# Forty weight columns in place of 64 in a state update, and fixed places in a scratch tile

## The chip, the cores and the metric

The kernel runs on one core of one Trainium2 chip. The metric is the device time of one execution in microseconds (us), taken as the median of several runs. Profiles are of one execution, and their times are counted from the start of its span.

## The reference

The whole program is an attention-like recurrence over 768 steps for 4 batches of 8 heads with 40 dimensions each, followed by two layers of a mixture of eight experts over the 3,072 tokens that come out of it. Only the recurrence matters for the change:

```python
    B, H, S, D = r.shape                       # 4, 8, 768, 40
    state = np.zeros((B, H, D, D), dtype=np.float32)
    for t in range(S):
        ...
        y[:, :, t] = np.einsum('bhd,bhde->bhe', rt, state)
        Sa = np.einsum('bhde,bhe->bhd', state, at)
        state_decay = state * wt[:, :, None, :] - np.einsum('bhd,bhe->bhde', Sa, bt)
        state = state_decay + np.einsum('bhd,bhe->bhde', vt, kt)
...
    x = np.ascontiguousarray(attn_out.transpose(0, 2, 1, 3)).reshape(B * S, H * D)
    x = _moe_ref(x=x, **moe_kwargs)
    return _moe2_ref(x=x, **moe2_kwargs)
```

The experts' part takes, for each token, one of eight experts by the largest logit, runs two matrix products with a ReLU between them, and scales the result by the expert's probability.

## The kernel before

The recurrence is done in 24 chunks of 32 steps. Within a chunk everything is a matrix product: the 32 steps' corrections to each other are gathered in a triangular system, whose inverse is needed for each of the 32 pairs of batch and head. Four chunks form a group, and there are six groups (0 to 5). The inverses of a group's four chunks are worked out together on VectorE, ahead of their use.

The order of the work is written out by hand: a loop over the chunks calls small functions in fixed places (slots), and VectorE work that has time is dealt out between them by a list with budgets (`Fill`). Each engine then works through its own instructions in that order and waits on semaphores where it needs another engine's result. So a slow step holds up everything behind it on its engine.

What is touched by the change:

- `z_` (L540 to L549) is the state update of a chunk on TensorE: 16 products into the PSUM tile `zps`, each with 64 columns of the tile `kb` as weights and two runs of 40 columns of `vu` moving. A head has 40 dimensions; its weights stand in 64 places of `kb`, 16 elements apart, and the last 24 places hold zeros. Two heads share the 128 PSUM partitions, one in the rows from 0, the other in the rows from 64. Each product is executed as two passes, so the profile shows 32 weight loads and 32 matmuls a chunk.
- `z_up` (L551 to L557) runs behind it on VectorE. It adds all 128 rows of `zps` to the state `zs` and scales by the chunk's decay. The next chunk's `x_z` (L523) needs the result. The path from chunk to chunk is thus `x_z` on TensorE, a copy on ScalarE, `u_` (L534), four scalings into `vu` on ScalarE (L538), `z_` (L549), and `z_up` on VectorE (L555, L557).
- Other steps on TensorE that the text names: `r_t` (L505) and `s_t` (L564) are transposes, `y_s` (L592), `y_c` (L602) and `c_` (L583) make the chunk's output, `chunk_a` (L333, L346, L358) prepares later chunks, `v_t` (L574) transposes `vu`.
- `solve` (L368 to L406) works out the inverses of groups 2 to 5; groups 0 and 1 go through another function, `Halves`. It has 31 steps `s`, each a product into the scratch tile `pr` (`t1`, L389) and a difference of it from the inverse's rows (`t2`, L395). In 27 of the 31 steps both are cut in two halves, so that the order is first product, second product, first difference, second difference. The text calls the place between the second difference of one step and the first product of the next a **seam**; there are 26 a group between steps that are cut, 104 in all.
- `pr` is taken anew from a pool with one buffer at each step, and the second half's product stands directly behind the first's in it.

At a seam the first product needs three things of the step before: the row `s + 1` of the inverse, which the first difference writes, the place in `pr`, and the tile itself, which the pool gives again when the last reader of the old one, the second difference, is done.

Of the kernel before, what the change touches and what calls it, by code (L numbers as in the profile page):

```python
# [11 lines left out]
F32 = mybir.dt.float32  # L12
# [4 lines left out]
P = 128  # L17
B, H, S, D = 4, 8, 768, 40
# [17 lines left out]
PRES = (0, 0, 7, 15, 15)  # L36
TAIL, SPREAD, AHEAD = 42, 60, (80, 91)
# [17 lines left out]
def attention(tc, zones, ident, r, k, v, w, a, b, emit_x, hook0, hook1, hook2, hook3, unsafe, extra, tail):  # L55
    nc = tc.nc
    with ExitStack() as ctx:
        cp = ctx.enter_context(tc.tile_pool(name="a_const", bufs=1))
        wp = ctx.enter_context(tc.tile_pool(name="a_work", bufs=2))
        ps = Warm(tc, ctx.enter_context(tc.tile_pool(name="a_psum", bufs=1, space=PSUM)), ident)  # L60

# [306 lines left out]
        def solve(st):  # L368
            box = {}
# [13 lines left out]

            def t1(s, a, z):
                am, tm = box["am"], box["tm"]
                if a == s + 1:
                    box["pr"] = wp.tile([P, 256], F32, name="pr", bufs=1)
                prv = box["pr"][:, (a - s - 1) * (s + 1) : (z - s - 1) * (s + 1)].rearrange("p (t j) -> p t j", j=s + 1)
                nc.vector.tensor_mul(prv, am[:, a:z, s : s + 1].to_broadcast([P, z - a, s + 1]),  # L389
                                     tm[:, s : s + 1, : s + 1].to_broadcast([P, z - a, s + 1]))  # L390

            def t2(s, a, z):
                tm = box["tm"]
                prv = box["pr"][:, (a - s - 1) * (s + 1) : (z - s - 1) * (s + 1)].rearrange("p (t j) -> p t j", j=s + 1)
                nc.vector.tensor_sub(tm[:, a:z, : s + 1], tm[:, a:z, : s + 1], prv)  # L395
# [12 lines left out]
        class Halves:  # L408
# [10 lines left out]
            def ops(self):  # L419
                am, tm, st, n = self.am, self.tm, self.st, L // 2  # L420

                def t0():
                    self.pr = wp.tile([P, 256], F32, name="pr", bufs=1)
                    for o in (0, n):
                        nc.vector.transpose(out=am[:, o : o + n], in_=st["aa"].rearrange("p h c t -> p t (h c)")[:, o : o + n])
# [67 lines left out]
        class Chunk:  # L493
# [46 lines left out]
            def z_(self):  # L540
# [3 lines left out]
                self.zps = zps = ps.tile([P, 2, 512], F32, tag="z", name="zps", bufs=1)  # L544
                for p in range(4):
                    for vv in range(2):
                        for i2 in range(2):
                            o = zps[64 * i2 : 64 * i2 + 64, vv, 0:320].rearrange("q (u p d) -> q u p d", u=2, p=4)[:, :, p]
                            nc.tensor.matmul(out=o, lhsT=kb[:, vv, i2, :, 4 * p + c], rhs=self.vuv[:, vv, :, 4 * i2 + p, :], start=True, stop=True, skip_group_check=True)  # L549
# [1266 lines left out]
```

## Time and profile before

| | |
|---|---|
| Median of 3 runs | 1023.16 us (1020.48 to 1031.33) |
| The profiled execution's own time | 1024.33 us |
| Its span, first to last instruction | 1022.1 us |
| Busy: TensorE matmul / weight load | 906.4 us / 838.8 us |
| Busy: VectorE / ScalarE / GpSimd | 706.1 / 506.6 / 304.7 us |
| Mean granted TensorE clock | 0.947 |

The span has two parts: the recurrence, up to about 500 us, and the experts behind it. The busy times are of the whole span. They say little of the change, which lies in the first part alone: there it has to be read stage by stage which engine waits for which.

### The profile page before, as it was taken

Reading aid. Unit: us, or ns where it says so; the run is one execution under the profiler, and the core shown is the slowest. Engines: PE = TensorE matmul, PEld = TensorE weight load, DVE = VectorE, ACT = ScalarE, POOL = GpSimd, SP = SyncE. Lnnn points to the kernel's source line nnn. Section 1 sums busy time; section 2 is a strip of 40 time slices with the busy share of each in tenths; the row PEclk is TensorE's granted clock in tenths of the full one; section 3 lists DMA queues with packets and bytes.
Section 4 is the critical chain, followed back from the end, with each engine's and each line's share of the span. In section 5 each row is a group of like instructions: output and inputs, shape, how many; then the busy total and the mean of one; then the engine's idle time right before and its main releaser. Section 6 shows DMA issues by size and latency. Waiting matters only on the chain. (4 is left out here: it accounts for less than half of the span.)

```text
span 1022.1 us, 38222 instructions
## 1 busy us (share of the span) xinstructions
PE 906.4 (89%) x16089; PEld 838.8 (82%) x16089; DVE 706.1 (69%) x2022; ACT 506.6 (50%) x991; POOL 304.7 (30%) x361
## 2 busy tenths in 40 slices
PE   7747988788878888988879899999999999999995
PEld 7646777677767777766769799999999999999995
DVE  7799899998996985853545354545464776766762
ACT  6625445445445577643523254444443565665662
POOL 6550021211120211112133334543543433323321
PEclk9779979998999999998989899999999999999998
DMA  5554445433532623226017434445343111271110
GB/s 175 141 136 111 73 107 108 116 90 79 98 86 47 159 51 87 50 51 158 17 28 173 124 97 134 129 106 152 101 126 97 30 40 53 79 214 42 40 41 26
DMA packets 152421, 96.41 MB, mean 94 GB/s; under 512 B 127407, under 2 KB 139585, under 8 KB 151850
## 3 DMA queue, kind: packets, MB, share of 16 engines
q1 hardware_dynamic: 138154, 72.53, 28.3%
q0 software_dynamic: 14080, 21.28, 8.1%
q8 instruction: 130, 2.13, 0.9%
q14 instruction: 57, 0.47, 0.1%
HBM read 112.18 MB, written 14.59 MB: 124 GB/s over the span
## 5 line engine op out<-in xcount | busy, mean ns | idle before, releaser
L1293 PE MATMUL hp<-xs,h 128*128 128x256 f32 (+1 forms) x840 | 157.1, 317 | 0.0
L1304 PE MATMUL yp<-h,hh 128*114 128x320 f32 (+1 forms) x464 | 146.9, 317 | 0.3 <-DMA s<-moe_w 0.3
L1305 PE MATMUL yp<-l,hh 128*114 128x320 f32 (+1 forms) x464 | 144.2, 311 | 0.0
L1306 PE MATMUL yp<-h,hl 128*114 128x320 f32 (+1 forms) x464 | 144.0, 310 | 0.0
L1296 DVE SCALAR_TENSOR_TENSOR hl<-hp,hh 128x456 fp32r<-128x456 f32 (+1 forms) x116 | 76.6, 660 | 90.9 <-ACT hh L1295 90.9
L1293 PEld LDWEIGHTS hp<-xs,h 128*128 128x128 f32 x840 | 124.6, 190 | 3.3
L1295 ACT ACTIVATE hh<-hp 128x456 fp32r<-128x456 f32 (+1 forms) x116 | 66.5, 573 | 110.8 <-PE hp L1293 106.2
L1293 PE MATMUL hp<-xs,l 128*128 128x256 f32 (+1 forms) x504 | 102.5, 312 | 0.0
L1214 DVE TENSOR_TENSOR l<-s,h 128x768 fp32r<-128x768 f32 x88 | 80.6, 956 | 13.1 <-ACT h L1213 10.8
L1304 PEld LDWEIGHTS yp<-h,hh 128*114 128x114 f32 (+1 forms) x464 | 85.3, 184 | 0.6 <-issue 0.5
L1305 PEld LDWEIGHTS yp<-l,hh 128*114 128x114 f32 (+1 forms) x464 | 85.3, 184 | 0.2
L1306 PEld LDWEIGHTS yp<-h,hl 128*114 128x114 f32 (+1 forms) x464 | 85.1, 183 | 0.0
L1293 PEld LDWEIGHTS hp<-xs,l 128*128 128x128 f32 x504 | 80.1, 190 | 3.1
L1249 POOL DMA_INDIRECT xg<-x,le x52 | 61.9, 1190 | 69.2 <-issue 58.0
L1220 DVE TENSOR_TENSOR l<-s,h 128x640 fp32r<-128x640 f32 x88 | 72.6, 825 | 3.0 <-ACT h L1219 3.0
L1361 POOL DMA_INDIRECT out<-yo,ti x28 | 34.5, 1232 | 129.2 <-ACT yo L1357 74.7
L1213 ACT CAST h<-s 128x768 fp32r<-128x768 f32 x88 | 70.4, 835 | 1.6 <-DMA s<-moe_w 1.5
L1219 ACT CAST h<-s 128x640 fp32r<-128x640 f32 x88 | 63.3, 719 | 0.0
L389 DVE TENSOR_TENSOR pr<-z_sol 128x110 f32<-128x110 f32 (+20 forms) x232 | 58.5, 282 | 3.9
L985 POOL TENSOR_TENSOR ccnt<-ccnt,oh 128x8 bf16<-128x8 bf16 x24 | 6.7, 279 | 179.5 <-PE rp L983 145.7
L1003 POOL DMA_INDIRECT lst<-l2e,posi x32 | 40.8, 1276 | 60.9 <-DVE posi L996 53.5
L1267 DVE TENSOR_TENSOR xs<-ta,xs 128x456 fp32r<-128x456 f32 (+1 forms) x28 | 18.5, 662 | 55.2 <-ACT xs L1266 55.2
(364 smaller groups left out, 1996.2 us busy)
## 6 DMA issues: line engine op xcount, KB each, us to landing
s<-moe_w SPq DMA_DIRECT2D x22, 1280.0 KB
s<-moe_w SPq DMA_DIRECT2D x22, 1024.0 KB
s<-moe_w SPq DMA_DIRECT2D x44, 256.0 KB
z_w<-w SPq DMA_DIRECT2D x40, 160.0 KB
z_kb<-k SPq DMA_DIRECT2D x24, 160.0 KB
z_kb<-b SPq DMA_DIRECT2D x24, 160.0 KB
z_pa<-a SPq DMA_DIRECT2D x96, 40.0 KB
rt<-r SPq DMA_DIRECT2D x96, 40.0 KB
```

Of the source, the lines that this page charges most:

```text
L389: nc.vector.tensor_mul(prv, am[:, a:z, s : s + 1].to_broadcast([P, z - a, s + 1]), tm[:, s : s + 1, : s + 1].to_broadcast([P, z - a, s + 1]))
L1213: nc.scalar.copy(wt["h1"][:, :, s], wt["s1"][:, :, s])
L1214: nc.vector.tensor_sub(wt["l1"][:, :, s], wt["s1"][:, :, s], wt["h1"][:, :, s].bitcast(F32))
L1219: nc.scalar.copy(wt["h2"][:, s], wt["s2"][:, s])
L1220: nc.vector.tensor_sub(wt["l2"][:, s], wt["s2"][:, s], wt["h2"][:, s].bitcast(F32))
L1249: d = self.nc.gpsimd.indirect_dma_start(out=b.xg[:, h], out_offset=None, in_=b.lay.src, in_offset=IndirectOffsetOnAxis(ap=b.le[:, h, 0:1]. ...
L1293: nc.tensor.matmul(out=hp[:, i], lhsT=l, rhs=r, start=k == 0, stop=k == len(ops) - 1)
L1295: nc.scalar.activation(hh[:, s], hp, AF.Relu)
L1296: nc.vector.scalar_tensor_tensor(out=hl[:, s], in0=hp, scalar=0.0, in1=hh[:, s].bitcast(F32), op0=ALU.max, op1=ALU.subtract)
L1304: nc.tensor.matmul(out=yp, lhsT=hh[:, k, t], rhs=wt["h2"][:, k], start=k == 0, stop=False)
L1305: nc.tensor.matmul(out=yp, lhsT=hh[:, k, t], rhs=wt["l2"][:, k], start=False, stop=False)
L1306: nc.tensor.matmul(out=yp, lhsT=hl[:, k, t], rhs=wt["h2"][:, k], start=False, stop=k == 7)
```

## The change

Three things are changed. The products of `z_` take the first 40 of a head's 64 weight columns, and so write 40 of its 64 PSUM rows. The PSUM tile that they write, now called `zz`, is taken once at the kernel's start and set to zero there on VectorE; `z_up` still reads all 128 rows of it. And `solve` takes its scratch tile once for a group's inverses and gives the first half's products the places from 0 and the second half's the places from 128, in every step; the tile grows from 256 to 264 elements.

```diff
+PR = 264
...
+        zz = ps.tile([P, 2, 512], F32, tag="z", name="zz", bufs=1)
+        nc.vector.memset(zz[:, :, :320], 0.0)
...
+            def place(s, a, z):
+
+                if "pr" not in box:
+                    box["pr"] = wp.tile([P, PR], F32, name="pr", bufs=1)
+                o = 128 if a > s + 1 else 0
+                return box["pr"][:, o : o + (z - a) * (s + 1)].rearrange("p (t j) -> p t j", j=s + 1)
+
             def t1(s, a, z):
                 am, tm = box["am"], box["tm"]
-                if a == s + 1:
-                    box["pr"] = wp.tile([P, 256], F32, name="pr", bufs=1)
-                prv = box["pr"][:, (a - s - 1) * (s + 1) : (z - s - 1) * (s + 1)].rearrange("p (t j) -> p t j", j=s + 1)
+                prv = place(s, a, z)
                 nc.vector.tensor_mul(prv, am[:, a:z, s : s + 1].to_broadcast([P, z - a, s + 1]),
                                      tm[:, s : s + 1, : s + 1].to_broadcast([P, z - a, s + 1]))
 
             def t2(s, a, z):
                 tm = box["tm"]
-                prv = box["pr"][:, (a - s - 1) * (s + 1) : (z - s - 1) * (s + 1)].rearrange("p (t j) -> p t j", j=s + 1)
+                prv = place(s, a, z)
                 nc.vector.tensor_sub(tm[:, a:z, : s + 1], tm[:, a:z, : s + 1], prv)
...
-                    self.pr = wp.tile([P, 256], F32, name="pr", bufs=1)
+                    self.pr = wp.tile([P, PR], F32, name="pr", bufs=1)
...
-                self.zps = zps = ps.tile([P, 2, 512], F32, tag="z", name="zps", bufs=1)
+                self.zps = zps = zz
                 for p in range(4):
                     for vv in range(2):
                         for i2 in range(2):
-                            o = zps[64 * i2 : 64 * i2 + 64, vv, 0:320].rearrange("q (u p d) -> q u p d", u=2, p=4)[:, :, p]
-                            nc.tensor.matmul(out=o, lhsT=kb[:, vv, i2, :, 4 * p + c], rhs=self.vuv[:, vv, :, 4 * i2 + p, :], start=True, stop=True, skip_group_check=True)
+                            o = zps[64 * i2 : 64 * i2 + D, vv, 0:320].rearrange("q (u p d) -> q u p d", u=2, p=4)[:, :, p]
+                            nc.tensor.matmul(out=o, lhsT=kb[:, vv, i2, 0:D, 4 * p + c], rhs=self.vuv[:, vv, :, 4 * i2 + p, :], start=True, stop=True, skip_group_check=True)
```

On VectorE, in the inverses of a group (first halves and second halves of the steps with 96, 99 and 108, and 110 elements; the name in brackets is VectorE's own semaphore, where the instruction waits on it), the kernel before has:

```order
L395 TENSOR_TENSOR z_sol<-z_sol,pr 128x13x7
L389 TENSOR_TENSOR pr<-z_sol 128x96 [waits DVE_49]
L389 TENSOR_TENSOR pr<-z_sol 128x96
L395 TENSOR_TENSOR z_sol<-z_sol,pr 128x12x8 [waits DVE_49] x2
L389 TENSOR_TENSOR pr<-z_sol 128x99 [waits DVE_49]
L389 TENSOR_TENSOR pr<-z_sol 128x108
L395 TENSOR_TENSOR z_sol<-z_sol,pr 128x11x9 [waits DVE_49]
L395 TENSOR_TENSOR z_sol<-z_sol,pr 128x12x9 [waits DVE_49]
L389 TENSOR_TENSOR pr<-z_sol 128x110 [waits DVE_49]
```

And the changed kernel has there:

```order
L403 TENSOR_TENSOR z_sol<-z_sol,pr 128x13x7
L397 TENSOR_TENSOR pr<-z_sol 128x96
L397 TENSOR_TENSOR pr<-z_sol 128x96 [waits DVE_49]
L403 TENSOR_TENSOR z_sol<-z_sol,pr 128x12x8 [waits DVE_49] x2
L397 TENSOR_TENSOR pr<-z_sol 128x99 [waits DVE_49]
L397 TENSOR_TENSOR pr<-z_sol 128x108 [waits DVE_49]
L403 TENSOR_TENSOR z_sol<-z_sol,pr 128x11x9 [waits DVE_49]
L403 TENSOR_TENSOR z_sol<-z_sol,pr 128x12x9 [waits DVE_49]
L397 TENSOR_TENSOR pr<-z_sol 128x110 [waits DVE_49] x2
```

No instruction has moved. What has moved is the wait: before, the first product of a step waits for the second difference of the step before, the instruction directly ahead of it, and the second product waits for nothing more. Now the first product depends on the first difference alone (its row and its places), two instructions back, and the second product on the second difference, also two instructions back.

On TensorE, around the state update of chunk 8 (`z_`, between the transposes of a later chunk and those of `v_t`), the kernel before has:

```order
L333 MATMUL aps<-ident,z_atok 128x128 x3
L549 MATMUL zps<-vu_146,kb_148 64x2x40 [waits DMAHW7_49,DMAHW6_49,Activation_49]
L549 MATMUL zps<-vu_146,kb_148 64x2x40
L549 MATMUL zps<-vu_146,kb_148 64x2x40 [waits DMAHW1_49,DMAHW0_49,Activation_49]
L549 MATMUL zps<-vu_146,kb_148 64x2x40 x13
L574 MATMUL vps<-ident,vu_146 80x64 [waits PE_49] x2
```

And the changed kernel has there:

```order
L336 MATMUL aps<-ident,z_atok 128x128 x3
L557 MATMUL zz<-vu_148,kb_150 40x2x40 [waits DMAHW7_49,DMAHW6_49,Activation_49]
L557 MATMUL zz<-vu_148,kb_150 40x2x40
L557 MATMUL zz<-vu_148,kb_150 40x2x40 [waits DMAHW1_49,DMAHW0_49,Activation_49]
L557 MATMUL zz<-vu_148,kb_150 40x2x40 x13
L582 MATMUL vps<-ident,vu_148 80x64 [waits PE_49] x2
```

Place, number and waits are the same; only the number of rows that each product writes is another.

## Rows read from the trace of the kernel before

**Rows 1.** The profile page: busy time by engine with instruction counts; the queue of instructions.

```profile
PE 906.4 (89%) x16089; PEld 838.8 (82%) x16089; DVE 706.1 (69%) x2022; ACT 506.6 (50%) x991; POOL 304.7 (30%) x361
...
q8 instruction: 130, 2.13, 0.9%
```

**Rows 2.** Windows: stretch and length, then each engine's busy time, clock, DMA share.

```profile
189.00:345.00 156.00, 128.62 (x4038) 111.72 (x4034) 140.78 (x421) 73.71 (x165) 28.80 (x38) 0.93 0.40 89
345.00:500.00 155.00, 132.84 (x4377) 114.12 (x4377) 98.21 (x373) 89.81 (x195) 26.66 (x43) 0.96 0.36 79
```

**Rows 3.** Windows over the inverses of groups 2 and 3, same columns.

```profile
184.28:236.35 52.07, 43.05 (x1257) 37.17 (x1261) 49.59 (x175) 21.37 (x48) 8.65 (x11) 0.88 0.41 97
258.80:312.20 53.40, 42.04 (x1290) 36.77 (x1291) 50.52 (x181) 24.18 (x53) 11.21 (x15) 0.94 0.44 90
```

**Rows 4.** Lines of VectorE, 184 to 440 us: count, busy us, mean ns, idle before.

```profile
L389 DVE TENSOR_TENSOR pr<-z_sol 128x110 f32<-128x110 f32 (+20 forms) x232 | 58.5, 282 | 3.9
```

**Rows 5.** Timeline of VectorE: two steps of an inverse (start us, length us).

```profile
269.73 0.43 DVE L389 TENSOR_TENSOR pr<-z_sol 128x96 f32<-128x96 f32 x2
270.07 0.42 DVE L395 TENSOR_TENSOR z_sol<-z_sol,pr 128x96 f32<-128x96 f32 x2
270.53 0.45 DVE L389 TENSOR_TENSOR pr<-z_sol 128x99 f32<-128x99 f32 x2
270.89 0.44 DVE L395 TENSOR_TENSOR z_sol<-z_sol,pr 128x99 f32<-128x99 f32 x2
```

**Rows 6.** Timeline of VectorE: behind the first and the last seam before 345 us.

```profile
197.89 0.41 DVE L389 TENSOR_TENSOR pr<-z_sol 128x84 f32<-128x84 f32 x2
...
343.00 0.41 DVE L389 TENSOR_TENSOR pr<-z_sol 128x84 f32<-128x84 f32 x2
```

**Rows 7.** Waits of VectorE, 189 to 345 us: total, times, longest.

```profile
DVE x L1654 <- PE yps L602: 4.3, 2, 3.8
```

**Rows 8.** Timeline of TensorE in chunk 8.

```profile
246.81 2.13 PE L549 MATMUL zps<-vu,kb 128*64 128x80 f32 x32
...
251.77 1.15 PE L583 MATMUL cps<-rb,vT 128*64 128x64 f32 x32
```

**Rows 9.** Timeline of TensorE in chunk 21, and the clock of that stretch.

```profile
474.51 2.40 PE L549 MATMUL zps<-vu,kb 128*64 128x80 f32 x32
...
474.40:477.00 2.60, 2.60 (x46) 2.35 (x42) 0.04 (x1) 0.00 (x0) 0.86 (x1) 0.54 0.45 74
```

**Rows 10.** Waits of TensorE, 345 to 500 us: total, times, longest.

```profile
PE zps L549 <- issue: 6.4, 4, 2.4
PE yps L592 <- issue: 5.6, 2, 4.1
PE xps L523 <- issue: 2.9, 5, 1.3
```

**Rows 11.** Timeline of TensorE in chunk 15.

```profile
374.41 0.70 PE L549 MATMUL zps<-vu,z_wide 128*64 128x80 f32 x8
377.47 1.87 PE L549 MATMUL zps<-vu,z_wide 128*64 128x80 f32 x24 [2.37 <-issue]
```

**Rows 12.** DMA queues (packets, MB, share): 374.5 to 377.6 us, then 340 to 500 us.

```profile
q8 instruction: 1, 0.02, 1.9%
...
q8 instruction: 35, 0.57, 1.6%
```

**Rows 13.** Timeline of VectorE in chunks 5 and 8.

```profile
188.04 0.82 DVE L555 TENSOR_TENSOR zs<-zps,zs 128x640 f32<-128x640 f32 x1 [0.61 <-PE zps L549]
...
248.99 0.82 DVE L555 TENSOR_TENSOR zs<-zps,zs 128x640 f32<-128x640 f32 x1 [2.06 <-PE zps L549]
```

**Rows 14.** Timeline of TensorE in chunk 16: transposes with 80 and with 128 weight columns.

```profile
388.12 0.60 PE L505 MATMUL rps<-ident,rt 128*80 128x128 f32 x4
388.56 0.62 PE L346 MATMUL kps<-ident,kb 128*128 128x128 f32 x4
```

**Rows 15.** Timeline of VectorE at the kernel's start.

```profile
9.08 0.24 DVE L269 TENSOR_TENSOR z_w<-z_w 128x80 f32<-128x80 f32 x1 [2.50 <-DMA z_w<-w]
```

## The prediction

> **What bounds the kernel now.** I read the page first, then windows, since the change lies in the first 500 us and the shares of the whole span hide it. There the recurrence has two stretches. Before 345 us the inverses of groups 2 to 5 stand on VectorE: it is busy 140.8 of 156.0 us [rows 2], and during the inverses of groups 2 and 3 themselves 49.6 of 52.1 and 50.5 of 53.4 us [rows 3]. The reader is to see that TensorE has room there (43.1 and 42.0 us), so a chunk of the recurrence is late because VectorE is. From 345 us no inverse is left, VectorE falls to 98.2 of 155.0 us, and TensorE with 132.8 us is the engine that the chain runs through [rows 2]. What idle time it has is put down mostly to "issue", time in which it waits for no other engine: 6.4 us before `z_`, 5.6 before `y_s`, 2.9 before `x_z` [rows 10]. The experts behind the recurrence are not touched and shift as a whole with its end.
>
> **The seams on VectorE.** What one costs is read in the timeline of an inverse [rows 5]. The pair of first products of one step begins at 269.73 and lasts 0.43, to 270.16; the differences begin at 270.07, which is 0.09 us earlier. Those last until 270.49, and the next step's products begin at 270.53, 0.04 us later; then again 270.53 + 0.45 = 270.98 against 270.89, 0.09 earlier. Inside a step each instruction depends on the one two places back, and VectorE overlaps it with the one between; at the seam it depends, through the tile, on the one directly ahead. The change makes the seam like the inside of a step, so it is worth 0.04 + 0.08 = 0.12 us (I take the smaller overlap). Against it stands that the second product now waits for the second difference; that too is two back, so it costs what the inside of a step costs, nothing more. The work of the products themselves (232 in the stretch from 184 to 440 us, 282 ns each [rows 4]) stays. The idle time charged to them there, 3.9 us, fits seams of about 0.04.
>
> Of the 104 seams 89 have nothing else of VectorE between the two steps: 22, 19, 23 and 25 in the four inverses. 46 of them lie before 345 us, the first ahead of 197.89, the last ahead of 343.00 [rows 6]. 46 x 0.12 = 5.5 us less of VectorE's time where it sets the end. Not all of that is kept: VectorE also waits there for TensorE (4.3 us for `yps` alone [rows 7]), and what it reaches sooner may wait longer. I take 4.5. The other 43 seams lie behind 345 us, where VectorE idles for 57 of 155 us: 0 of their 5.2 us. If VectorE were the limit there after all, they would come on top; rows 2 exclude most of that.
>
> **The state update on TensorE.** Its 32 passes take 2.13 us, the 32 of `c_` with 64 contiguous weight columns and 64 moving ones 1.15 us [rows 8]. Two reasons could make `z_` dear: 80 moving columns, or the load of 64 weight columns that lie 16 elements apart. Chunk 21 tells them apart. There the granted clock was 0.54, about the lower of TensorE's two levels (1.2 and 2.4 GHz); the group took 2.40 us, 13% more than at the full clock [rows 9]. Moving columns at half the clock would take nearly twice as long. So at the full clock the load sets the pace, 2.13 / 32 = 67 ns for 64 columns, and with 40 columns the group takes 2.13 x 40 / 64 = 1.33 us if the load goes by columns. The moving part may hold it higher: from `c_`, 1.15 x 80 / 64 = 1.44 us. That saves 0.7 to 0.8 us a chunk, and I take 0.7. The lower bound is 0: four transposes with 80 weight columns took 0.60 us, four with 128 columns 0.62 [rows 14], so a load does not always set the pace in proportion. Below nothing lies only the case of rival D. In a stretch at the lower clock I take 0, since the columns moved set the time there.
>
> The Trainium skill, page "TensorE: Matmul & The Clock Gate", section "LDWEIGHTS (loading the stationary operand)", gives a load as its columns divided by 1.2 in nanoseconds. By that, an estimate, 24 columns fewer save 20 ns a load and 0.64 us a chunk, and the sum below would be shorter by nearly the same. The trace's 67 ns is above the page's 53 for 64 columns, so strides or the rest of the pass cost something besides.
>
> Where does this count? Before 345 us only where VectorE waits for `zps`: in chunk 8 the addition of `z_up` was held up for 2.06 us by `z_`, in chunk 5 for 0.61 [rows 13]. There the saving of 0.7 and all 0.6 are kept, 1.3 us; in the others VectorE is late anyway. From 345 to 500 us `z_` lies on the chain in nine chunks (14 to 22), 9 x 0.7 = 6.3 us at most. But TensorE has another limit there. In chunk 15 it stopped within `z_`, after 8 of 32 passes, for 2.37 us, with no wait on anybody [rows 11]. In these 3.1 us one packet landed on the queue of instructions [rows 12]. The page counts 130 such packets of together 2.13 MB, and 16,089 matmuls and as many loads, 32,178 / 130 = 248 to a packet [rows 1]; from 340 to 500 us there were 35, one per 4.6 us [rows 12]. So I read "issue" as TensorE waiting for its own program, which comes at a rate that the shorter passes don't raise: their number stays. An engine that gets through `z_` sooner reaches the end of what has been delivered sooner. How much of 6.3 us is swallowed is bounded by 0 and 6.3; the idle sums of rows 10 (14.9 us over nine chunks, 1.7 a chunk, more than twice the saving) say that most stretches between stops are held by it; that `z_` itself was stopped only 4 times says that some aren't. I take half: 3.1 us.
>
> **The rest.** Setting `zz` to zero is one instruction on VectorE, 640 elements wide, as wide as the addition of 0.82 us [rows 13]. It stands at the start, where VectorE waits 2.50 us for a weight's DMA [rows 15]: 0, and 0.8 if that cover is gone. The products keep their number, places and waits, and the sum over `zz` is as wide as before: 0. With one `zz` for all chunks, the next `z_` waits for the last read of it by `z_up`, as with a pool of one buffer: 0. `Halves` gets a scratch tile 8 elements larger: 0.
>
> **The sum.** 4.5 + 1.3 + 3.1 = 8.9 us, so 1024.33 - 8.9 = 1015.4 us. The profiled execution is 1.2 us above the median of the runs shown, inside their scatter; I keep its own time.
>
> **The rivals.**
> A, the forecast: between 1011.5 and 1018.5, by how much of the two terms is swallowed. Chance 0.50.
> B: "issue" isn't a fixed rate, and the state updates pay fully. Then 5.5 (no seam's gain lost) + 1.3 + 6.3 = 13.1 us: 1011.2, and down to 1007 if seams behind 345 us count too. For it: the chain does pass through `z_` in each chunk, and rows 10 name only four stops directly before it. Against it: rows 11 and 12. 0.22.
> C: the shorter load gives nothing, because the strided read or the moving columns pace it or the stops take all. Then 4.5 alone: 1019.8. For it: 35 packets at an even rate; against it: chunk 21's 13%. 0.14.
> D, the other side: a product that writes 40 of 64 rows no longer runs beside its neighbour in the other half of the array, and passes that now overlap go one behind the other. A pass would go from 67 to at most twice that, 2.1 us more a chunk, on 11 chunks of the path 23 us, with 4.5 off for the seams 1043. It decides from 4.5 / (11 x 32) = 13 ns more a pass. For it: nothing in the trace shows a product with 40 columns. Against it: 80 of 128 columns were no dearer than 128 [rows 14]. 0.06.
> E: the change doesn't do what it says on VectorE. The gap at a seam belongs to an instruction's own end and not to the wait, and the seam stays: 1024.33 - 1.3 - 3.1 = 1019.9. Against it: the same engine, the same widths, and 0.12 us between dependent one and two back [rows 5]. 0.08.
>
> The Trainium skill speaks for E: its page "VectorE: DVE Perf Modes", section "The DRAIN you can't avoid", finds 8 chained copies as long with a semaphore after each as without, and advises to cut operations, not semaphores. Rows 5 differ, by 0.12 us between two kinds of dependence; by the page alone the first term would be 0.
>
> **How the numbers follow.** The likeliest case gives 1015.4. The range, 8 in 10: C and E, 1019.8 and 1019.9, take it up to 1021, with 1 us for the scatter; D stays outside (0.06). Downward B's 1011 is in and its tail to 1007 half out: 1008. One per cent, 10.2 us, is about what a measurement of this kernel can tell from no change; that is 1012.9 counted from the median. Below it lie most of B (0.19) and an edge of A (0.08): faster 0.27. D alone is slower, 0.05 of its 0.06 beyond the bound. The rest, 0.68, is within.
>
> **What would show it.** In the timeline of an inverse, seams that begin 0.08 us ahead of the last difference's end in place of 0.04 behind it, and inverses of groups 2 and 3 about 2.5 us shorter each. The group of 32 `z_` passes near 1.4 us where the clock is full, 2.4 in any at the lower one. "Issue" before `z_`, `y_s` and `x_z` grown by some 3 us over the nine chunks, with 35 packets as before. The recurrence's end about 9 us earlier. I would be wrong with `z_` at 2.1 us or above (C, D), with the seams unmoved (E), or with "issue" unchanged and the whole 6.3 us at the end (B); also if VectorE, done sooner with an inverse, only waits longer for `yps`.

## The result and the profile after

The changed kernel takes 1010.62 us (median of 4 runs, 1001.13 to 1016.44) beside 1021.82 us for the kernel before (4 runs, 1015.85 to 1031.33; one more than the three above); the ratio is 0.988, 95% interval 0.983 to 0.993, or 12.3 us less with 7 to 17 in the interval. The ratio leaves out executions more than 1.5% above the fastest of their kernel, here the slowest one of each, so it is not the quotient of these medians. Timed once more (below) the ratio was 0.9879. The forecast was 8.9 us less. The execution that was profiled took 1014.81 us.

First VectorE's timeline in an inverse of the changed kernel (start us, length us), at the same steps as [rows 5]:

```profile
264.69 0.42 DVE L397 TENSOR_TENSOR pr<-z_sol 128x96 f32<-128x96 f32 x2
265.03 0.42 DVE L403 TENSOR_TENSOR z_sol<-z_sol,pr 128x96 f32<-128x96 f32 x2
265.37 0.44 DVE L397 TENSOR_TENSOR pr<-z_sol 128x99 f32<-128x99 f32 x2
265.72 0.44 DVE L403 TENSOR_TENSOR z_sol<-z_sol,pr 128x99 f32<-128x99 f32 x2
```

The differences end at 265.03 + 0.42 = 265.45, and the next step's products begin at 265.37, 0.08 us earlier; before they began 0.04 us later. Two steps take 1.38 us from 264.69 (to 266.07, where the next begins) in place of 1.63 from 269.73. All 89 seams with nothing else between look like this: the product begins 0.076 to 0.090 us ahead of the difference's end, before 0.034 to 0.035 behind it. The windows over the inverses of groups 2 and 3 (columns as in [rows 2]):

```profile
183.03:230.62 47.59, 40.57 (x1291) 34.72 (x1291) 46.52 (x175) 22.13 (x50) 11.68 (x11) 0.89 0.45 108
254.68:305.80 51.12, 39.78 (x1259) 34.32 (x1262) 48.33 (x180) 23.96 (x52) 13.08 (x15) 0.92 0.43 92
```

They are 4.5 and 2.3 us shorter than [rows 3], and VectorE's busy time in them is 3.1 and 2.2 us less, for 22 and 19 seams. Next TensorE's timeline of the changed kernel, the state updates of chunks 8 and 21 and the products of `c_`, which are unchanged; then the window of the last of them:

```profile
242.35 1.41 PE L557 MATMUL zz<-vu,kb 128*40 128x80 f32 x32
...
248.26 1.15 PE L591 MATMUL cps<-rb,vT 128*64 128x64 f32 x32
...
463.63 2.37 PE L557 MATMUL zz<-vu,kb 128*40 128x80 f32 x32
```

```profile
463.63:466.00 2.37, 2.37 (x38) 2.16 (x36) 0.00 (x0) 0.00 (x0) 0.73 (x1) 0.50 0.43 69
```

Against [rows 8] the 32 passes fell from 2.13 to 1.41 us. Where the granted clock is 0.50, the lower of the two levels, they take 2.37 us, as good as the 2.40 of before [rows 9]. TensorE's waits from 345 to 500 us in the changed kernel (total, times, longest) answer to [rows 10]:

```profile
PE zz L557 <- issue: 6.1, 2, 3.2
PE yps L600 <- issue: 5.9, 2, 4.4
PE xps L531 <- issue: 2.1, 3, 1.4
```

These three make 14.1 us in place of 14.9. The windows do not hold quite the same chunks (chunk 14 begins at 351.64 before and at 342.74 here); the idle time is added up by chunks below. Last, windows of the late part cut by chunks instead of as a whole, of the kernel before (chunks 17 to 19, then 20 to 22):

```profile
400.61:443.59 42.98, 38.99 (x1286) 32.97 (x1286) 37.39 (x159) 27.36 (x60) 5.99 (x9) 1.00 0.30 50
443.59:497.17 53.58, 42.72 (x1293) 36.21 (x1292) 20.65 (x70) 22.49 (x50) 10.73 (x21) 0.90 0.37 91
```

and the same chunks in the changed kernel:

```profile
391.16:431.64 40.48, 36.42 (x1287) 30.66 (x1287) 34.90 (x159) 27.36 (x60) 6.25 (x9) 1.00 0.32 53
431.64:486.72 55.08, 43.56 (x1292) 36.89 (x1291) 20.61 (x70) 22.39 (x50) 10.73 (x21) 0.81 0.37 88
```

The reader is to see two unlike stretches that my single window from 345 to 500 us had mixed. In chunks 17 to 19 TensorE (38.99) and VectorE (37.39) are both nearly full in 42.98 us, and 2.5 us are gained there. In chunks 20 to 22 VectorE has room (20.65 of 53.58), TensorE's mean clock went from 0.90 to 0.81 and 1.5 us were given back. That is one execution of each: in the second profile of the changed kernel the same two stretches take 42.24 and 55.83 us.

One warning for all such readings: the second profile of the changed kernel has the recurrence's last chunk begin at 497.32 us, the first at 486.72, and the kernel before at 497.17. So the start of one late chunk in one profile cannot show a difference of 10 us; the durations of single groups can be compared, and what a change is worth to the whole kernel is read from many executions.

### The profile page after: what moved, and what is told of

Read it like the earlier page. It is cut to its first block, busy times and chain, and to the rows that moved or that the text cites. A ratio compares the mean times of both kernels' runs of the same rounds, so it can differ in the third digit from the quotient of the medians.

```text
span 1012.6 us, 38223 instructions
## 1 busy us (share of the span) xinstructions
PE 896.7 (89%) x16089; PEld 828.0 (82%) x16089; DVE 695.9 (69%) x2023; ACT 506.5 (50%) x991; POOL 308.8 (30%) x361
## 3 DMA queue, kind: packets, MB, share of 16 engines
q8 instruction: 130, 2.13, 0.9%
## 5 line engine op out<-in xcount | busy, mean ns | idle before, releaser
L1275 DVE TENSOR_TENSOR xs<-ta,xs 128x456 fp32r<-128x456 f32 (+1 forms) x28 | 18.5, 662 | 55.6 <-ACT xs L1274 55.4
L1274 ACT CAST xs<-ta 128x456 fp32r<-128x456 f32 (+1 forms) x28 | 15.8, 564 | 79.3 <-PE ta L1271 79.3
```

## Experiments

**Each part alone.** The places without the columns (the state update as before):

```diff
-        zz = ps.tile([P, 2, 512], F32, tag="z", name="zz", bufs=1)
-        nc.vector.memset(zz[:, :, :320], 0.0)
...
-                self.zps = zps = zz
+                self.zps = zps = ps.tile([P, 2, 512], F32, tag="z", name="zps", bufs=1)
...
-                            o = zps[64 * i2 : 64 * i2 + D, vv, 0:320].rearrange("q (u p d) -> q u p d", u=2, p=4)[:, :, p]
-                            nc.tensor.matmul(out=o, lhsT=kb[:, vv, i2, 0:D, 4 * p + c], rhs=self.vuv[:, vv, :, 4 * i2 + p, :], start=True, stop=True, skip_group_check=True)
+                            o = zps[64 * i2 : 64 * i2 + 64, vv, 0:320].rearrange("q (u p d) -> q u p d", u=2, p=4)[:, :, p]
+                            nc.tensor.matmul(out=o, lhsT=kb[:, vv, i2, :, 4 * p + c], rhs=self.vuv[:, vv, :, 4 * i2 + p, :], start=True, stop=True, skip_group_check=True)
```

> The fixed places alone; the state update as before (64 weight columns, its PSUM tile taken anew). My steps: every seam begins 0.08 us ahead of the difference before it in place of 0.04 behind it, 46 of them count, the time falls by 4.5 us (ratio 0.9956), the chunk that starts near 352 us starts 4 to 6 us earlier, and nothing more is gained behind it. Rival: the gap belongs to the instruction, the seams stay at +0.03 and the ratio at 1.000. Second rival, from the trace of the changed kernel, in which that chunk starts 8.9 us earlier: VectorE's path pays more than once, and the seams alone bring 7 us or more (ratio 0.993 or less).

Measured: 0.9946 (0.9916 to 0.9975), 5.5 us less. My 4.5 us hold, and the 46 x 0.12 = 5.5 before my deduction hold better; "7 us or more" (0.993 or less) is inside the interval too and not excluded. The instruction's own gap (1.000) is. One step that I expected does not show: the chunk near 352 us begins at 351.01 in this kernel's profile, 0.6 us earlier than before and not 4 to 6. In the two profiles of the changed kernel it begins at 342.74 and 352.30, so that one profile cannot tell either way.

The columns without the places (the same three pieces put into the kernel before):

> The 40 weight columns in the cleared tile alone; the scratch tile of the inverses as before. My steps: a group of 32 passes takes 1.44 us, 1.3 us are gained before 345 us and 3.1 of 6.3 us behind it, ratio 0.9957, with idle time put down to issue in the stretch of the last nine chunks larger than before. Rival (issue is no limit): 6.3 us behind 345 us, ratio 0.9926. Rival (all of it swallowed): ratio 0.9985 or above.

Measured: 0.9977 (0.9944 to 1.0011), 2.3 us less. The full 6.3 us behind 345 us (0.9926) lie outside. My 4.4 lie inside, as does nothing at all. The same kernel again:

> The 40 weight columns alone, the same kernel as in the second run, timed again to narrow the interval. If the two parts add up to the changed kernel's 0.988 beside the places' 0.9946: 0.993. If the first reading holds (most of the saving behind 345 us is swallowed): 0.996 to 0.998.

Measured: 0.9983 (0.9944 to 1.0023), 1.7 us less. Both readings say about 2 us, half of what I took. The idle time put down to issue, which I expected to grow, is taken up below. And the changed kernel again:

> The changed kernel as it is, timed beside the same runs of the kernel before. By the two parts alone (ratios 0.9946 and 0.9977) the sum is 0.992; by its first four runs 0.988. If the two parts add up, 0.990 to 0.993; if each pays more beside the other, 0.986 to 0.989.

Measured: 0.9879 (0.9836 to 0.9923), the lower of the two expectations, with both in the interval. 5.5 and 2.0 us make 7.5, the whole gives 12.3. The intervals overlap (a sum of 8 to 10 us is inside all of them), so that the parts pay more together is suggested and not shown.

**A third dose of the wait.** Within a step, each half's product with its difference behind it; the columns as before:

```diff
-                for f in (t1, t2):
-                    for a, z in halves(s):
+                for a, z in halves(s):
+                    for f in (t1, t2):
                         ops.append(lambda f=f, s=s, a=a, z=z: f(s, a, z))
```

> As the kernel with the fixed places alone, but within a step each half's product and its difference stand next to each other, so that two instructions a step wait for the one directly ahead, in place of none (one in the kernel before). If what costs is that wait, each such place begins 0.03 us behind and not 0.08 ahead, and a step takes 0.23 us more than with the fixed places, 0.12 more than before: with 46 of 89 places before 345 us that is 5 us above the kernel before (ratio about 1.005), more if VectorE's path pays more than once. If the gap belongs to the second difference or to the step's first product, the time is that of the fixed places alone (0.996).

Measured: 1.0056 (1.0017 to 1.0096), 5.7 us more. Its VectorE timeline:

```profile
274.09 0.25 DVE L395 TENSOR_TENSOR pr<-z_sol 128x96 f32<-128x96 f32 x1
274.38 0.26 DVE L401 TENSOR_TENSOR z_sol<-z_sol,pr 128x96 f32<-128x96 f32 x1
274.55 0.25 DVE L395 TENSOR_TENSOR pr<-z_sol 128x96 f32<-128x96 f32 x1
274.84 0.26 DVE L401 TENSOR_TENSOR z_sol<-z_sol,pr 128x96 f32<-128x96 f32 x1
```

274.09 + 0.25 = 274.34, and the dependent difference begins at 274.38, 0.04 us later; 274.38 + 0.26 = 274.64, and the next product, which does not depend on it, begins at 274.55, 0.09 us earlier. With none, one and two such waits a step the time is -5.5, 0 and +5.7 us (intervals -8.6 to -2.6 and 1.7 to 9.8): steps of one size, each about 47 times 0.12 us. This settles the seams: it is the dependence on the instruction directly ahead, not the instruction.

**What a pass of the state update costs.** The changed kernel with 16 further products behind `z_`, in five forms from chunk to chunk (chunk number modulo 5), their results not read:

```diff
...
+                kind = self.cc % 5
+                n = (64, 64, D, 24, D)[kind]
+                m = 1 if kind == 4 else 2
...
+                            wide = kb[:, vv, i2].rearrange("q e n -> q (e n)")
+                            left = wide[:, 64 * p : 64 * p + n] if kind in (1, 2) else kb[:, vv, i2, 0:n, 4 * p + c]
+                            nc.tensor.matmul(out=t[64 * i2 : 64 * i2 + n, : m * D].rearrange("q (u d) -> q u d", u=m), lhsT=left,
+                                             rhs=self.vuv[:, vv, 0:m, 4 * i2 + p, :], start=True, stop=True, skip_group_check=True)
```

> The changed kernel with 16 further products behind those of the state update in each chunk, into a PSUM tile that nobody reads, in five forms that take turns from chunk to chunk: 64 strided weight columns and 80 moving; 64 contiguous and 80; 40 contiguous and 80; 24 strided and 80; 40 strided and 40. If the number of weight columns sets the pace: 2.1, 2.1, 1.4, 1.4 (or less), 1.3 us for the 32 passes. If it is the stride: 2.1, 1.4, 1.4 (or less), 1.4 and 1.3. If with 40 columns the moving side already sets it: the second to fourth forms at 1.44 wherever the load is shorter, the last at about 0.8 to 1.0. The time of the kernel is of no interest.

TensorE's timeline (one execution, in stretches at the full clock); the rows are of chunks 3, 7 (the kernel's own group, then the further one), 14, 15 and 16:

```profile
150.12 1.32 PE L571 MATMUL xps<-vu,z_wide 128*24 128x80 f32 x32
...
235.52 1.44 PE L557 MATMUL zz<-vu,z_wide 128*40 128x80 f32 x32
236.78 1.28 PE L571 MATMUL xps<-vu,z_wide 128*40 128x80 f32 x32
...
367.42 1.31 PE L571 MATMUL xps<-vu,z_wide 128*40 128x40 f32 x32
...
386.27 1.98 PE L571 MATMUL xps<-vu,z_wide 128*64 128x80 f32 x32
...
402.39 1.28 PE L571 MATMUL xps<-vu,z_wide 128*64 128x80 f32 x32
```

64 strided columns take 1.98 us (1.98 to 2.13 in the four such chunks at the full clock), 64 contiguous ones 1.28, as do 40 contiguous. So the stride makes the load dear. 40 strided columns take 1.31 us with half the moving columns: there the load still sets the pace, and 1.98 x 40 / 64 = 1.24 is near it. About 1.3 is also what 80 moving columns need, since 24 strided columns take 1.32 and contiguous ones 1.28. With 40 strided and 80 moving both are equal, and the group takes 1.44, a little above either.

The Trainium skill, page "TensorE: Matmul & The Clock Gate", section "LDWEIGHTS (loading the stationary operand)", has the load go by the number of columns alone, columns divided by 1.2 in nanoseconds; an estimate by it is 53 ns for 64. By these rows the number alone does not decide: 64 contiguous columns go through in at most 1.28 us / 32 = 40 ns a pass, the same 64 with a stride of 16 elements in 62.

**Is it the program's delivery?** 32 small products (128 instructions) behind `z_` in chunks 14 to 22 of the changed kernel:

```diff
...
+                for _ in range(32):
+                    nc.tensor.matmul(out=t[:16, :16], lhsT=ident[:, :16], rhs=ident[:, :16], start=True, stop=True, skip_group_check=True)
```

> The changed kernel with 32 small products (16 weight columns, 16 moving, results not read) behind the state update of the chunks 14 to 22: 64 passes and 64 loads, 128 instructions a chunk, half a packet of the instruction queue. By their own duration, at most that of the 64 passes of the state's first product (0.80 us), they cost 9 x 0.8 = 7 us at the most, and the stops of TensorE stay. If the delivery of the program is what limits those chunks, half a packet costs 4.6 / 2 = 2.3 us at the mean rate of before, 1.7 at the shortest distance seen, so 15 to 21 us in nine chunks, ratio 1.003 to 1.009 to the kernel before in place of 0.988 to 0.995, with more idle time put down to issue.

Measured: 1.0074 (1.0046 to 1.0102), 20 us above the changed kernel: as the delivery theory had it. But my bound on the products' own duration was wrong; in this kernel's timeline of TensorE the 64 passes take 1.76 us, or 9 x 1.76 = 16 us:

```profile
360.61 1.76 PE L565 MATMUL xps<-ident 128*16 128x16 f32 x64
```

So both theories were still in. The same time in 24 instructions tells them apart:

```diff
-                for _ in range(32):
-                    nc.tensor.matmul(out=t[:16, :16], lhsT=ident[:, :16], rhs=ident[:, :16], start=True, stop=True, skip_group_check=True)
+                for n in (P, P, P, P, P, 24):
+                    nc.tensor.matmul(out=t[:, :n], lhsT=ident, rhs=ident[:, :n], start=True, stop=True, skip_group_check=True)
```

> The changed kernel with 6 large products (128 weight columns, five with 128 and one with 24 moving columns, results not read) at the place where the 32 small ones stood, in chunks 14 to 22: about the same 1.7 us of TensorE's time, but 24 instructions in place of 128. If what the small ones cost (20 us above the changed kernel) was the delivery of their instructions, these cost clearly less: 0 to 8 us, ratio 0.988 to 0.996, with idle time put down to issue smaller than in the changed kernel, since the program arrives meanwhile. If it was their own 1.7 us on the path, the cost is the same 9 x 1.7 = 15 us, ratio 1.003 or more.

Measured: 1.0075 (1.0036 to 1.0114), the same. The timeline has 1.52 us for the group; the queue of instructions has 130 packets, where the small products had brought it to 135:

```profile
371.32 1.52 PE L565 MATMUL xps<-ident 128*128 128x128 f32 x12
```

104 instructions a chunk more cost nothing that these runs can see. What costs is TensorE's time: an added 1.5 to 1.8 us is paid at least in full, nine times. (Both kernels lose 20 us, 4 to 6 more than the groups' own duration; the intervals allow for that, and what it is was not found.) So a delivery of the program at a fixed rate, at which every instruction has its price, falls as the reason why a saving would be lost. The one packet per 4.6 us from which I had taken the rate is what the kernel uses, not what the queue can bring.

The stops themselves are waits for the program all the same, and the profiles show it. In chunk 20 of the kernel before TensorE stopped once in `u_` and once in `z_`, after 25 of its 32 passes:

```profile
450.07 0.70 PE L534 MATMUL ups<-xs,tt 32*32 32x40 f32 x33 [1.27 <-issue]
...
456.23 0.80 PE L549 MATMUL zps<-vu,kb 128*64 128x80 f32 x7 [2.11 <-issue]
```

In the changed kernel it stopped after the same 25 passes, for longer:

```profile
445.10 0.76 PE L557 MATMUL zz<-vu,kb 128*40 128x80 f32 x7 [3.22 <-issue]
```

And from one stop of the kernel before to the next lie as many instructions (windows, columns as in [rows 2]; matmuls and loads are the numbers behind the first two times):

```profile
445.11:450.06 4.95, 3.69 (x127) 3.06 (x126) 0.49 (x1) 2.52 (x5) 1.63 (x6) 1.00 0.22 21
450.07:456.22 6.15, 3.99 (x127) 3.46 (x127) 3.43 (x25) 1.71 (x4) 1.30 (x6) 1.00 0.33 69
```

With the few records of TensorE's sequencer that is 256, to within one. All stops over 1 us between 60 and 505 us that are put down to issue, 16 in that profile and 12 in the changed kernel's, lie whole multiples of 256 such records apart, to within one; a packet of the queue holds about as many, 248 matmuls and loads [rows 1]. The stop within `z_` of chunk 20 ends 1.4 to 1.5 us after such a packet has landed, at 454.80 us before and at 443.64 in the changed kernel. So a stop has its place in the program, whatever the passes take.

How long it lasts varies. The one in `z_` of chunk 16 took 1.53 us before, 2.86 and 1.4 in the two profiles of the changed kernel, 2.9 in one of the columns alone and less than 0.4 in the other; that of chunk 15 (2.37 us before) is missing from the changed kernel's. All idle time of TensorE that is put down to issue in chunks 14 to 22 adds up to 19.0 us before, 18.6 and 18.5 in the changed kernel, 16.8 and 19.7 with the columns alone, but 9.5 in the kernel with two waits a step. That it grows with shorter passes is thus neither shown nor excluded.

**Other work taken away.** Without the filler products ahead of `y_s` in chunks 17 to 23 (taken out of the table that sets them):

```diff
-(17, 'yps', 0): 2, (18, 'yps', 0): 2, (19, 'yps', 0): 2, (20, 'yps', 0): 2, (21, 'yps', 0): 2, (22, 'yps', 0): 2, (23, 'yps', 0): 1
```

> The changed kernel without the two filler products (4 passes, 0.69 us) that stand ahead of the chunk's output product in chunks 17 to 22, and the one in 23: 52 instructions fewer. If TensorE's own work sets the end there: 0.7 us on up to seven chunks, 4 us below the changed kernel. If the passes only fill the wait for the scaled corrections, or a wait for the program: no difference. If without them TensorE's clock falls more often: slower than the changed kernel by 2 us or more.

Measured: 0.9899 (0.985 to 0.9948), no difference from the changed kernel's 0.988. The 4 us less (0.984) lie just outside the interval; the 2 us more of my third case lie inside it and are not excluded. A part of the work removed stood ahead of a wait: TensorE's `z_` waited 2.5 us in all for ScalarE's scaling into `vu` between 345 and 500 us, in the changed kernel 0.9:

```profile
PE zz L557 <- ACT vu L546: 2.5, 4, 1.2
```

The state update in halves, ordered so that VectorE's first addition needs half of the products:

```diff
-                for p in range(4):
-                    for vv in range(2):
+                for vv in range(2):
+                    for p in range(4):
...
-                nc.vector.tensor_add(zn.rearrange("p (a b) -> p a b", a=2), self.zps[:, :, :320], self.zf.rearrange("p (a b) -> p a b", a=2))
                 zx = zn.rearrange("q (x d) -> q x d", d=D)
-                nc.vector.tensor_mul(zx, zx, nqlf[:, nc_].rearrange("q b p -> q (b p)").unsqueeze(2).to_broadcast([P, 16, D]))
+                qx = nqlf[:, nc_].rearrange("q b p -> q (b p)").unsqueeze(2)
+                for a in range(2):
+                    nc.vector.tensor_add(zn[:, 320 * a : 320 * a + 320], self.zps[:, a, :320], self.zf[:, 320 * a : 320 * a + 320])
+                for a in range(2):
+                    xa = zx[:, 8 * a : 8 * a + 8]
+                    nc.vector.tensor_mul(xa, xa, qx[:, 8 * a : 8 * a + 8].to_broadcast([P, 8, D]))
```

> The changed kernel, with the state update ordered by the two halves of its PSUM tile, and the addition and the scaling on VectorE each cut in two halves of 320 elements. The first addition can begin when half of the products are done, and the last scaling ends 1.2 us after them in place of 1.7. If time between chunks is saved where TensorE has no wait of its own: 0.5 us on nine chunks, 4 to 5 us below the changed kernel (ratio 0.983 to the kernel before). If TensorE's waits for its program swallow half, 2 us (0.986). If the four instructions in place of two cost VectorE more than they save before 345 us: equal to the changed kernel or up to 2 us above it (0.988 to 0.990).

Measured: 0.9891 (0.9853 to 0.9928), equal to the changed kernel. In the one chunk whose timeline was read, chunk 14, the latency that I shortened is on nobody's path: VectorE's two halves and scalings ran from 356.75 to 358.43, and TensorE, at work in its own order since `z_` ended at 354.58 but for two waits of 0.5 us together, began the next `x_z` at 360.07:

```profile
356.75 0.88 DVE L566 TENSOR_TENSOR zs<-zz,zs 128x320 f32<-128x320 f32 x2
357.55 0.88 DVE L569 TENSOR_TENSOR zs<-zs,qlf 128x320 f32<-128x320 f32 x2
```

**The same principle elsewhere.** In the changed kernel, from chunk 4 on, an instruction of the inverse or the decays put between dependent ones in the choice of an expert, its row, and `z_up`; `gap()` issues one and charges it to the list's budget:

```diff
         nc.vector.reduce_max(out=mx, in_=lp, axis=AX.X)
+        gap()
         nc.vector.tensor_sub(d, lp, bc(mx))
         nc.scalar.activation(ex, d, AF.Exp)
+        gap()
...
```

> The changed kernel with the same principle at three further places on VectorE: between the five dependent small operations that choose a token's expert, the three that give its row, and the addition and the scaling of the state update, one instruction of the inverse or of the decays that has time is put, from chunk 4 on, and taken off what the list deals out next. Nothing is computed otherwise. If a dependence on the instruction directly ahead costs 0.12 us wherever it stands, about seven places a chunk save 0.8 us on the nine chunks in which VectorE sets the end: 5 to 8 us below the changed kernel, ratio 0.980 to 0.983. If these places cost nothing (small operations wait for something else) or a later routing result holds up TensorE: 0.988 or above.

Measured: 0.9893 (0.9848 to 0.9937), no gain beside the changed kernel; 0.983 and below lie outside. Its timeline of VectorE shows that the spacing itself works:

```profile
212.06 0.15 DVE L996 TENSOR_TENSOR dl<-lp,mx 128x8 f32<-128x8 f32 x1
212.14 0.27 DVE L404 TENSOR_TENSOR pr<-z_sol 128x120 f32<-128x120 f32 x1
212.33 0.15 DVE L999 SCALAR_TENSOR_TENSOR tb<-dl,rev 128x8 f32<-128x8 f32 x1
```

Each begins 0.07 to 0.08 us ahead of the end before it. So these places got shorter and the kernel did not; what took their place was not found.

**The late seams.** The changed kernel with the fixed places in groups 2 and 3 alone:

```diff
-                if "pr" not in box:
-                    box["pr"] = wp.tile([P, PR], F32, name="pr", bufs=1)
-                o = 128 if a > s + 1 else 0
+                late = st["g"] >= 4
+                if "pr" not in box or (late and a == s + 1 and box.get("step") != s):
+                    box["pr"], box["step"] = wp.tile([P, PR], F32, name="pr", bufs=1), s
+                o = (a - s - 1) * (s + 1) if late else 128 if a > s + 1 else 0
```

> The changed kernel (40 weight columns everywhere), with the fixed places in the inverses of groups 2 and 3 alone; in those of groups 4 and 5 the scratch tile is taken anew in each step, as before, so that their 48 seams, 43 of them behind 345 us, wait for the instruction directly ahead again. By my prediction these seams are worth nothing: equal to the changed kernel but for 5 seams, 0.988 to 0.989. Rival, by the windows of chunks 17 to 19 (TensorE busy 39.0 and VectorE 37.4 of 43.0 us before): both engines are nearly full there, and neither part pays without the other; then 43 x 0.12 = 5 us go, and with them what the columns gain there: ratio 0.993 or more.

Measured: 0.9911 (0.9874 to 0.9948). Both expectations lie in the interval, and 0.9911 is between them: inconclusive.

The profiles say more. Nearly all 43 late seams lie in chunks 14 to 19. Windows over these six chunks, columns as in [rows 2], first with 64 weight columns: the kernel before and the one with two waits a step:

```profile
351.64:443.59 91.95, 82.97 (x2782) 71.59 (x2782) 69.06 (x274) 62.98 (x137) 13.80 (x20) 0.98 0.33 64
357.48:448.94 91.46, 83.39 (x2782) 72.14 (x2782) 72.43 (x279) 63.19 (x137) 14.33 (x20) 0.96 0.33 64
```

Then with 40: the changed kernel in its two profiles, the columns alone in theirs, and this kernel; the last three have the wait at the late seams:

```profile
342.74:431.64 88.90, 79.10 (x2783) 67.75 (x2783) 65.94 (x277) 63.10 (x137) 14.18 (x20) 0.98 0.35 67
352.30:441.49 89.19, 79.66 (x2783) 67.80 (x2783) 63.95 (x266) 63.00 (x135) 13.76 (x20) 0.98 0.33 65
354.12:442.78 88.66, 79.64 (x2782) 67.50 (x2782) 68.80 (x275) 62.98 (x137) 13.80 (x20) 1.00 0.34 66
347.81:437.92 90.11, 79.15 (x2783) 68.04 (x2783) 68.58 (x275) 63.23 (x137) 13.83 (x20) 0.98 0.33 65
343.56:433.07 89.51, 80.65 (x2782) 68.08 (x2782) 69.54 (x279) 63.09 (x137) 13.79 (x20) 0.98 0.34 66
```

The late seams cost VectorE 2.6 to 5.6 us of busy time here, but the stretch is as long with them (88.7 to 90.1 us) as without (88.9 and 89.2). The rival's 5 us do not show. The columns do: 88.7 to 90.1 us, 89.3 in the mean, in place of 91.5 and 92.0. That is 2.4 us of the 6 x 0.7 = 4.2 that the shorter groups save. It rests on seven single executions, in which the lengths of one kind lie within 1.5 us.

## Why the prediction was right, and where a step of it was not

**What bounds the kernel.** "From 345 us no inverse is left" was false, and contradicts the 43 seams that the same text puts there: the inverses of groups 4 and 5 run to 437 us. I had read one window for the late part, saw VectorE idle for 57 of 155 us, and gave its seams nothing. Cut by chunks, 33 of those 57 us lie in chunks 20 to 22, and in 17 to 19 VectorE is nearly as full as TensorE. My 0 for the late seams was right in size all the same: over chunks 14 to 19 VectorE's 2.6 to 5.6 us do not shorten the stretch, in which it has some 20 us to spare. The timed ratio (0.9911) leaves it open.

**The seams.** Right in mechanism, 0.12 us each, and in size: 46 x 0.12 = 5.5 against 5.5 measured (2.6 to 8.6). My deduction to 4.5 for longer waits is neither shown nor excluded. That the gap is the instruction's own (rival E) is excluded by three doses: here the dependence on the instruction directly ahead is worth 11.2 us between none and two a step. So the finding of the Trainium skill that I cited, in the section "The DRAIN you can't avoid" of its page "VectorE: DVE Perf Modes", that a semaphore behind each of 8 chained copies costs nothing, does not carry over to these seams; a chain like the page's was not run here.

**The group of passes.** 1.44 us was my upper value, from `c_`, and 1.41 to 1.44 was measured; 0.7 a chunk is right, as is 0 at the lower clock. That the load sets the pace is right, with the stride as its reason, which I had named beside the number of columns but not separated. Rivals C and D, as far as they rest on the pass, fall with the 1.41 us. That the stops swallow all of the saving, the rest of C, lies inside the intervals of the columns alone, but not beside the 2.4 us of chunks 14 to 19.

**How much of it counts.** 4.4 us (1.3 + 3.1) were predicted for the columns; alone they gave 2.3 and 1.7, with 4.4 and nothing inside both intervals, so the size is not excluded but probably too large. Of the 3.1 behind 345 us, chunks 14 to 19 show about the half that I took, 2.4 of 4.2; chunks 20 to 22 scatter from 46 to 56 us and show nothing. The 1.3 before 345 us were not told from the scatter: VectorE waited 2.1 us for `z_` between 189 and 345 us before, 1.3 and 3.0 in the two profiles of the changed kernel, 1.9 and 1.3 with the columns alone.

The step that failed is the reason for the half. That the stops put down to "issue" are waits for the program was right: they stand 256 instructions apart. That the program comes at a rate which sets the pace was not: I had read the kernel's own use of one packet in 4.6 us as the queue's limit, and 104 instructions a chunk more cost nothing. That "issue" grows by 3 us did not show (19.0 us before, 18.6 and 18.5 after). What does take the other half of the saving was not found. B, that the state updates pay fully, is excluded for the columns alone (0.9926 is outside), and chunks 14 to 19 speak against it; by the times it is not excluded beside the places, where the changed kernel stands 6.7 us below the places alone.

**The sum.** 8.9 us against 12.3 (7 to 17): sign and range right. But a range from 1008 to 1021 us holds C, E and most of B as well, and 12.3 is nearer to B's 13.1 than to 8.9; the total alone would have shown none of the steps. The 3.4 us between are less than the intervals. If they are real, they are the two parts' effect on each other (alone they make 7.5). The stretch with two full engines does not explain that: with 40 columns chunks 14 to 19 are as long without the late places as with them. Where else it could lie stays open.

**The rest.** The setting of `zz` to zero takes 0.59 us and ends at 1.62 us of the span, with a wait of VectorE for a DMA still behind it. It, the larger tile and the unmoved order cost nothing that shows.

## What to carry to other kernels

On VectorE, put one independent instruction between two that depend on each other; a scratch buffer that is taken again in each step is such a dependence too, though no data pass through it. That shortens VectorE; it shortened the kernel where VectorE sets the end, and not at the late seams. Make the weights of a matrix product contiguous, or load fewer of them when they are strided (here fp32, 16 elements apart; a strided moving side was not tested). Before you call a stop a wait for the program, count the instructions from one stop to the next. And cut the windows of a profile by the stages of the work before giving an engine "room": an average over a full stretch and an idle one is true of neither.

## What the runs showed of the hardware

A VectorE instruction that depends on the one directly ahead of it begins 0.03 to 0.04 us after that one's end. If it depends on the one two back, it begins 0.07 to 0.09 us before the end of the one between. Both were seen with 8 elements and with about 100.

A load of 64 fp32 weight columns 16 elements apart held a pass at 62 ns, the same number of contiguous columns at 40 ns or less. A pass with 128 rows, 16 weight columns and 16 moving ones still took 27 ns (1.76 us for 64), while the 64 passes of `x_z`, with the same 128 rows and more columns, 32 as weights and 40 moving, come at 13 ns (0.80 us). So a small product is not cheap by its size. One difference is that the passes of `x_z` write four blocks of 32 PSUM rows in turn and the small ones all the same 16 rows; whether that is the reason was not tested.

TensorE's program comes in packets, and TensorE stops for them at places 256 instructions apart: all stops over 1 us in the recurrence that no other engine explains, 16 in the kernel before and 12 in the changed one, lie at such places. The stop that was read closely ended 1.4 to 1.5 us after a packet had landed.

Chunks 20 to 22 took 53.58 us in the kernel before, 55.08 in the changed one, and in the kernel with two waits a step 47.16 (here), though nothing of its work there differs from the kernel before:

```profile
448.94:496.10 47.16, 40.43 (x1293) 34.45 (x1292) 20.47 (x71) 22.43 (x50) 10.78 (x21) 0.93 0.42 103
```

In the kernel with the early places alone it took 46.13, in the second profile of the changed one 55.83. So this stretch alone scatters by 8 to 10 us, more than most of the effects studied here. In the kernel with two waits its granted clock was 0.93, in the kernel before 0.90 and in the changed one 0.81, and TensorE idled 6.7 us in place of 10.9 and 11.5. What decides it in an execution was not found.
